# A five-stage pipeline for the weight conversion, with its sign mask in PSUM, and another order of the expert loop and the changeover

## Chip, core and metric

One core of a Trainium2 chip runs the whole program. The metric is device time in microseconds (us), the median over runs; less is better. TensorE (PE) multiplies matrices into PSUM; VectorE (DVE), ScalarE (ACT) and GpSimd (POOL) do elementwise work; SyncE (SP) issues most transfers. Each engine executes its own queue in order and waits for the others by semaphores.

## What is computed

Attention with queries averaged in pairs, then two feed-forward layers ("expert layers") on 1152 tokens of width 512, with 2048 hidden units. The reference, cut:

```python
q_pool = q.reshape(B, H, S // 2, 2, D).mean(axis=3)          # B=2, H=8, S=1152, D=64
attn = softmax(q_pool @ k^T / 8);  out = attn @ v
x = out as (1152 tokens, 512)
h = x @ w_in;   x = np.maximum(0.01 * h, h) @ w_out           # layer 0: 512 -> 2048 -> 512
h = x @ w_in2;  x = (h * np.tanh(softplus(h))) @ w_out2       # layer 1, same sizes
```

The four weight matrices arrive as 64-bit floats; everything else is 32-bit.

## The kernel before, in words

**Attention.** Eight pairs of heads, nine tiles of 128 queries each, so tiles 0 to 71. A tile n goes through scores on PE (tokens A, B, S, L263), maxima on DVE (M, N, K), the exponential on ACT (X, L290), three groups of transposes on PE (T, L311), and for each group a rounded copy on ACT (H, L319) and the remainder on DVE (L, L323). The product with the values (L339) ends in an ACT copy (L349), a small transfer and a POOL addition (L352). The queues' order is written out by hand, as strings of tokens: PATTERN for the first seven pairs, LAST for the eighth, TAIL behind it. PATTERN isn't touched. LAST and TAIL, the changeover, mix the last pair with the first expert work and the first weight blocks.

**Expert layers.** A layer takes its tokens in chunks of 512, 320 and 320 and, for each chunk, 16 hidden slices of 128. An iteration `it` (0 to 95) is one slice of one chunk: W, the in-projection, 12 matmuls into one of four PSUM banks (L552); u, two activations on ACT (L564, L565), of which one writes a rounded copy in a ring of three buffers and one rewrites the bank; y, a DVE subtraction that leaves the remainder (L567); O, the out-projection, 12 matmuls into four accumulators (L575). W reads X and the in-weights, O the u and y of its iteration and the out-weights. The string MOE says in which order one pass through the loop emits them: W(i), O(i-3), y(i-2), u(i), then Z, the copies at a chunk's end. u(i) writes the buffer that O(i-3) reads, so it waits for O(i-3).

**Weight conversion (class Conv).** 64 blocks of 128 x 512 weights, 32 per layer, in the order in which W and O need them. Per block: a 512 KB load (SP, L464); `ca`, two ACT instructions that take the high and the low word apart (L475, L476); `cv`, two DVE instructions that cut out the sign bit (L488) and put it on the shifted high word (L490); `cm`, a POOL addition of the low word (L503); `ch`, a rounded copy on ACT (L515); `cl`, the remainder, on DVE or POOL (L523). A "tick" emits the next step of each. Blocks 0 to 7 (`i < NA`) use one set of scratch buffers in I, later ones another in F. RATE says how many ticks a pass emits in the three stretches where blocks are converted: chunk 0 of layer 0 (2.25 a pass), chunk 2 of layer 0 (1.5, already for layer 1, whose weights overwrite layer 0's), chunk 0 of layer 1 (1).

The ring of buffers for late blocks, and the test for the start of a block:

```python
return tail[0], itmp[2 + i % 2], tail[1 + i % 2]          # one y, two k, two a
if i >= self.loaded or i > self.vecs or (self.merged < i if i < NA else self.merged < i - 1):
    return
```

Of the kernel before, what the change touches and what calls it, by code (L numbers as in the profile page):

```python
# [28 lines left out]
NA = 8  # L29
RATE = (2, 2.25, 1.5, 1)  # L30
# [11 lines left out]
    "B2 P70 X1 T00 P50 A2 H00 T20 H20 M2 S2 L00 T01 S3 A3 B3 N2 T10 H01 L20 K2 H10 T11 pv L01 X2 T21 L10 H21 T22 M3 N3 A4 K3 H22 L21 B4 H11 X3 L22 M4 T02 T12 H02 S4 H12 B5 L02 T23 L12 cf A5 H23 T03 L11 P20 N4 P120 K4 P30 ca P10 X4 cv c M5 P10 S6 H03 L23 ca T13 ch cp S5",  # L42
    "T11 L00 N2 T01 H01 H11 A3 B3 cv K2 X2 L01 T21 M3 N3 H21 H10 L21 cm L10 A4 B4 S4 ca ch cp T22 H22 L11 E0 P80 K3 P70 cv c X3 L22 P40 T02 H02 M4 N4 L02 T12 K4 T13 A5 H12 ca cv H13 ch T03 L13 cl L12 S5 X4 B5 H03 M5 N5 T23 c T14 ch cp ca H14 cv K5 L03 H23 W cm X5 T05 ch cp L14 ca L23 H05 cv c ch E0 P180 cl P10 T04 W T24 H04 L04 L05 T15 ca u c H15 T25 I5 H25 ch cp L25 ca u cv cm W ch cp H24 y W u B6 y L15 P190 W K6 R L24 M6 S6 O u A6 y X6 O N6",
    "A4 N4 K4 M4 S4 B4",
]
TAIL = "ca cv W ca cv u c cm ch y cl ca O cv ch cm cl y W ca u cv ch cl cm ca cv ch cl Y O u ca c cm ch cl ca cv ch cm cl"
MOE = "W O y u Z"
# [3 lines left out]
def tile_attention_moe_moe(  # L51
# [18 lines left out]
    F = sb.tile([128, 6432], F32, name="F")  # L70
# [186 lines left out]

    def emit_s(n, which):
        p = n // 9
        ops = q_ops(n)  # L260
# [27 lines left out]
    def emit_x(n):  # L288
        a, e = S_ALL[n % 2]
        nc.scalar.activation(out=ebuf[n % 3], in_=PS[:, a:e], func=AF.Exp, scale=SCALE,  # L290
                             bias=mx[:, n % 3, 2:3], accum_out=rcol(n))

    t_free, t_src = [0, 1, 2], {}
# [13 lines left out]
    def emit_t(n, g):  # L307
        bank, col = t_take()
        for i in range(3):
# [20 lines left out]
    def pv_ops(p, u):  # L330
# [40 lines left out]
    def last_recip():  # L371
        for first, c0, n in ((True, 0, 256), (False, 256, 320)):
# [17 lines left out]
    def pair_end_ops(p):  # L390
# [5 lines left out]
        def part(c0, n, first):  # L396
            bank, col = t_take()
# [30 lines left out]
    class Conv:  # L428


        def __init__(self):
            self.blocks = by_need(0) + by_need(1)
            self.loaded = self.acts = self.vecs = self.merged = self.highs = self.lows = 0
# [16 lines left out]
        def load(self):  # L450
            while self.loaded < len(self.blocks):
                i = self.loaded
                used = min(self.acts, self.vecs)
                if i < NA:
                    free = i - 2 < used
                elif i < NA + 3:
                    free = used >= NA and (i < NA + 2 or self.lows >= NA)
                else:
                    free = i - 3 < used
                if not free:  # L460
                    return
# [4 lines left out]
                self.loaded += 1  # L466

        def begin_act(self):
            i = self.acts
            if i >= self.loaded or i > self.vecs or (self.merged < i if i < NA else self.merged < i - 1):  # L470
                return
            y, k, a = self.bufs(i)
            if wide:
                v = self.raw(i).rearrange("p (n t) -> p n t", t=2)
# [3 lines left out]
            self.acts += 1  # L478

        def begin_vec(self):  # L480
            i = self.vecs
            if i >= self.acts or i - 2 >= self.lows:
                return
            y, k, a = self.bufs(i)
            if wide:
                ai = a.bitcast(I32)
                high = self.raw(i).rearrange("p (n t) -> p n t", t=2)[:, :, 1]
# [256 lines left out]
```

## Time and profile before

| | us |
|---|---|
| median of 3 runs | 694.49 (693.28 to 694.6) |
| profiled execution | 694.62 |
| its span, first to last instruction | 692.8 |
| PE busy / DVE busy / ACT busy / POOL busy | 659.6 / 442.8 / 428.7 / 280.8 |

The attention takes about the first 262 us, the expert layers the rest. A busy PE is not PE at its peak: matmuls are pipelined, and a row of 12 that waits in its middle shows as longer. The distance between the starts of two rows of PE says more: a W or an O of 12 matmuls takes 2.72 us for 512 tokens and 1.76 us for 320 where nothing holds it.

### The profile page before, as it was taken

What the parts mean: (1) busy time and instruction counts of PE and PEld (TensorE: products, weight loads), DVE (VectorE), ACT (ScalarE), POOL (GpSimd) and SP (SyncE); (2) the same over time, 40 slices, a digit from 0 to 9 for tenths busy, and PEclk for the clock granted to TensorE, in tenths of its full rate; (3) what the DMA queues carried; (4) which work ended last, traced back from release to release, by engine and by line L of the source; (5) the groups of instructions that cost most, each with busy time, mean ns of one, the idle gap of its engine ahead of it and who ended that gap; (6) DMA issues with size and microseconds to landing.
All of it is one profiled execution on the core that took longest, in us unless ns stands there. A gap on an engine that the chain in (4) does not pass through costs nothing. (4 is left out here: it accounts for less than half of the span.)

```text
span 692.8 us, 11045 instructions
## 1 busy us (share of the span) xinstructions
PE 659.6 (95%) x4048; PEld 599.3 (86%) x4048; DVE 442.8 (64%) x784; ACT 428.7 (62%) x851; POOL 280.8 (41%) x239
## 2 busy tenths in 40 slices
PE   2999999999999989989989999998999999999997
PEld 1899999999999867867768999998788889999997
DVE  5889999999999897499993111499975622111111
ACT  4989999898999797668773222477965422222221
POOL 6768577686857356465550000055532200000000
PEclk9999999999999999999999999999999999999999
DMA  6233232323322233355550000055532101001001
GB/s 170 73 83 115 81 105 90 82 80 84 114 78 52 70 115 113 111 167 183 182 184 28 1 1 1 31 184 183 167 137 91 31 1 61 1 1 39 1 1 39
DMA packets 18167, 57.74 MB, mean 83 GB/s; under 512 B 2368, under 2 KB 5440, under 8 KB 18112
## 3 DMA queue, kind: packets, MB, share of 16 engines
q1 hardware_dynamic: 16992, 52.44, 23.3%
q0 software_dynamic: 1120, 4.59, 2.9%
q8 instruction: 32, 0.52, 0.3%
q14 instruction: 23, 0.19, 0.1%
HBM read 47.71 MB, written 2.36 MB: 72 GB/s over the span
## 5 line engine op out<-in xcount | busy, mean ns | idle before, releaser
L575 PE MATMUL PS<-R 128*128 128x320 f32 (+1 forms) x1152 | 219.7, 339 | 7.5 <-DVE R L567 5.3
L552 PE MATMUL PS<-R 128*128 128x320 f32 (+1 forms) x1152 | 219.2, 339 | 1.2 <-ACT R L515 0.6
L575 PEld LDWEIGHTS PS<-R 128*128 128x128 f32 x1152 | 186.3, 188 | 28.5 <-DVE R L567 6.8
L552 PEld LDWEIGHTS PS<-R 128*128 128x128 f32 x1152 | 189.2, 190 | 18.3 <-DVE R L523 1.7
L564 ACT ACTIVATE R<-PS 128x320 fp32r<-128x320 f32 (+1 forms) x96 | 46.9, 489 | 187.8 <-PE PS L575 168.9
L503 POOL TENSOR_TENSOR F<-F,I 128x512 int32<-128x512 int32 x56 | 86.1, 1537 | 178.5 <-DVE F L490 174.2
L567 DVE TENSOR_TENSOR R<-PS,R 128x320 fp32r<-128x320 f32 (+1 forms) x96 | 52.6, 553 | 134.3 <-ACT PS L565 130.7
L263 PE MATMUL PS<-R 128*128 128x512 f32 (+2 forms) x480 | 110.5, 360 | 14.4 <-DVE R L213 9.5
L323 DVE TENSOR_TENSOR R<-PS,R 128x384 fp32r<-128x384 f32 x216 | 113.3, 550 | 11.2 <-ACT R L319 7.6
L319 ACT CAST R<-PS 128x384 fp32r<-128x384 f32 x216 | 95.0, 489 | 13.8 <-PE PS L311 11.9
L311 PE MATMUL PS<-F 128*128 128x128 f32 x648 | 95.1, 275 | 5.4 <-DVE R L323 4.1
L263 PEld LDWEIGHTS PS<-R 128*128 128x128 f32 x480 | 76.2, 193 | 22.9 <-issue 13.7
L290 ACT ACTIVATE F<-PS,F 128x1152 f32<-128x1152 f32 x72 | 88.6, 1231 | 10.1 <-PE PS L263 5.7
L339 PE MATMUL PS<-R 128*128 128x256 f32 (+1 forms) x576 | 93.8, 304 | 0.3 <-ACT R L319 0.2
L311 PEld LDWEIGHTS PS<-F 128*128 128x128 f32 x648 | 76.6, 140 | 15.4 <-DVE R L323 4.8
L339 PEld LDWEIGHTS PS<-R 128*128 128x128 f32 x576 | 80.0, 189 | 1.8 <-DVE R L323 0.5
L271 DVE TENSOR_REDUCE F<-PS 128x1 f32<-128x896 f32 x72 | 77.9, 1082 | 4.3 <-PE PS L263 4.3
L137 POOL TENSOR_TENSOR R<-I,R 64x1152 fp32r<-64x1152 f32 (+1 forms) x28 | 57.3, 2047 | 1.6
L523 DVE TENSOR_TENSOR R<-F,R 128x512 fp32r<-128x512 f32 x56 | 48.2, 860 | 14.7 <-ACT R L515 14.5
L488 DVE TENSOR_SCALAR F<-I 128x512 int32<-128x512 int32 x56 | 55.1, 984 | 2.8 <-POOL F L352 2.0
L490 DVE SCALAR_TENSOR_TENSOR F<-F 128x512 int32<-128x512 int32 x56 | 41.0, 733 | 24.7 <-ACT F L475 19.8
L352 POOL TENSOR_TENSOR F<-F 64x256 f32<-64x256 f32 (+1 forms) x32 | 25.9, 808 | 56.5 <-DMA F<-F 29.2
(75 smaller groups left out, 464.2 us busy)
## 6 DMA issues: line engine op xcount, KB each, us to landing
I<-in_w_dram SPq DMA_DIRECT2D x64, 512.0 KB, 3.3
I<-in_vN_dram SPq DMA_DIRECT2D x8, 576.0 KB, 4.2
R<-R POOLq DMA_DIRECT2D x14, 320.0 KB, 4.2
I<-in_qT_dram SPq DMA_DIRECT2D x7, 576.0 KB, 4.8
I<-in_kT_dram SPq DMA_DIRECT2D x7, 576.0 KB, 4.0
F<-F SPq DMA_DIRECT2D x16, 80.0 KB, 2.0
out_dram<-I SPq DMA_DIRECT2D x8, 160.0 KB, 2.0
F<-F SPq DMA_DIRECT2D x16, 64.0 KB, 1.9
```

The costliest lines, as they stand in the source:

```text
L137: nc.gpsimd.tensor_tensor(out=out, in0=src, in1=rounded(top), op=ALU.subtract)
L263: nc.tensor.matmul(out=PS[:, pc:pc + w], lhsT=lq, rhs=KS[p % 2][:, h, kc:kc + w], start=(i == 0), stop=(i == len(ops) - 1))
L271: nc.vector.tensor_reduce(out=mx[:, n % 3, 0:1], in_=PS[:, a:e], axis=AX.X, op=ALU.max, negate=True)
L290: nc.scalar.activation(out=ebuf[n % 3], in_=PS[:, a:e], func=AF.Exp, scale=SCALE, bias=mx[:, n % 3, 2:3], accum_out=rcol(n))
L311: nc.tensor.transpose(PS[:, col + 128 * i:col + 128 * i + 128], ebuf[n % 3][:, 128 * k:128 * k + 128], ident)
L319: nc.scalar.copy(out=pt_dst(n, g, 0), in_=t_src[n, g][1])
L323: nc.vector.tensor_tensor(out=pt_dst(n, g, 1), in0=src, in1=rounded(pt_dst(n, g, 0)), op=ALU.subtract)
L339: nc.tensor.matmul(out=PS[:, bank[1]:bank[1] + n], lhsT=vs[:, k, 128 * h:128 * h + 128], rhs=PT[:, slot, s, k, 0:n], start=(k == 0 and s = ...
L488: nc.vector.tensor_scalar(out=ai, in0=high, scalar1=-2 ** 31, scalar2=None, op0=ALU.bitwise_and)
L503: nc.gpsimd.tensor_tensor(out=a.bitcast(I32), in0=a.bitcast(I32), in1=k.bitcast(I32), op=ALU.add)
L552: nc.tensor.matmul(out=out, lhsT=wi[:, ws, k, fs], rhs=X[:, xs, k, tk], start=(k == 0 and i == 0), stop=(k == KD - 1 and i == 2))
L575: nc.tensor.matmul(out=PS[:, ACC[d]:ACC[d] + w], lhsT=wo[:, ws, f % FPS, 128 * d:128 * d + 128], rhs=G[:, it % 3, gs, 0:w], start=(f == 0 ...
```

## The change

Conv becomes one `step(what)` for five stages (act, vec, merge, high, low; the tokens ca, cv, cm, ch, cl now mean one step each), with a table of free buffers. A tick runs the stages from the last to the first, so each stage in a tick works on another block. Late blocks have two y, three k and four a buffers, in the place of the attention's exponentials. From block 10 on the sign bit (L533 in the new code) is written to PSUM bank 3, and the following instruction (L535) reads it there; the in-projection then rotates over three banks. LAST, TAIL and MOE have another order, and RATE is counted in half passes: 2, 1.25 and 1.2 ticks a pass. Weights of slices 4 to 7 and expert steps on blocks from 8 on are held back until the attention's end. `after()` and PT_FREE only assert an order while the program is built; they emit nothing.

```diff
-RATE = (2, 2.25, 1.5, 1)
+RATE = (1, 0.625, 0.6)
...
-MOE = "W O y u Z"
+MOE = "W O Z u t y t"
...
-    tail = [F[:, 800 + i * 512:1312 + i * 512] for i in range(3)]
+    cy = [F[:, 2976 + i * 512:3488 + i * 512] for i in range(2)]
+    ck = [F[:, 4000 + i * 512:4512 + i * 512] for i in range(3)]
+    signs = PS[:, 1536:2048].bitcast(I32)
+    ca = [F[:, 5536:6048], F[:, 6432:6944], itmp[2], itmp[3]]
...
-            return tail[0], itmp[2 + i % 2], tail[1 + i % 2]
+            j = i - NA
+            return cy[j % 2], ck[j % 3], ca[j % 4]
+        def free(self, i, what):
+            d = self.done
+            used = min(d["act"], d["vec"])
+            early = {"load": (2, used), "act": (1, min(d["vec"], d["merge"])), "vec": (2, d["low"])}
+            late = {"load": (3, used), "act": (2, min(d["vec"], d["merge"] + 1)), "vec": (4, d["low"])}
+            if what not in early:
+                return True
+            if i >= NA:
+                n, given = late[what]
+                if what == "load" and i < NA + 3:
+                    return given >= NA and (i < NA + 2 or d["low"] >= NA)
+                if what == "act" and t_count[0] < 3 * NT or what == "vec" and i > NA + 1 and d["merge"] < NA:
+                    return False
+                return i < NA + n or i - n < given
+            n, given = early[what]
+            return i - n < given
...
-                nc.vector.tensor_scalar(out=ai, in0=high, scalar1=-2 ** 31, scalar2=None,
+                sign = signs if cnt["y"] > 3 else ai
+                nc.vector.tensor_scalar(out=sign, in0=v[:, :, 1], scalar1=-2 ** 31, scalar2=None,
                                         op0=ALU.bitwise_and)
-                nc.vector.scalar_tensor_tensor(out=ai, in0=y.bitcast(I32), scalar=3, in1=ai,
+                nc.vector.scalar_tensor_tensor(out=ai, in0=y.bitcast(I32), scalar=3, in1=sign,
                                                op0=ALU.logical_shift_left, op1=ALU.bitwise_or)
...
         def tick(self):
             self.load()
-            self.begin_act()
-            self.begin_vec()
-            self.high()
-            self.merge()
-            self.low(nc.vector)
+            for what in reversed(self.STAGES):
+                self.step(what)
...
-    HB = [0, 512, 1024, 1536]
+    def h_bank(it):
+        return 512 * (it % 4 if it <= 4 else (it - 4) % 3)
...
+            if it >= (cnt["y"] + (4 if it <= 4 else 3) if t == "W" else cnt[{"u": "W", "y": "u", "O": "y"}[t]]):
+                return
+            parts = {"W": (0, 1), "O": (2 + ITS[it][2] % FPS,)}.get(t, ())
+            if not conv.open and any(conv.index(it, b) >= max(NA, conv.lows) for b in parts):
+                return
```

**What moves: DVE in a pass of chunk 0 of layer 0.** First the kernel before, then the changed one, each from a y on (L567 and L602 are y; L488/L490 and L533/L535 are cv; L523 and L552 are cl).

```order
L567 TENSOR_TENSOR R<-PS,R 128x512
L488 TENSOR_SCALAR F<-I 128x512
L490 SCALAR_TENSOR_TENSOR F<-F 128x512
L523 TENSOR_TENSOR R<-F,R 128x512
L488 TENSOR_SCALAR F<-I 128x512
```

```order
L602 TENSOR_TENSOR R<-PS,R 128x512
L552 TENSOR_TENSOR R<-F,R 128x512
L533 TENSOR_SCALAR PS<-I 128x512
L535 SCALAR_TENSOR_TENSOR F<-F,PS 128x512
L552 TENSOR_TENSOR R<-I,R 128x512
```

Two blocks a pass in both; now cl (of an older block) stands ahead of cv, and the sign goes through PS.

**ACT at tiles 67 to 69 of the last pair**, before and changed. L290 and L306 are the exponential, L349 and L373 the copies of the value products, L319 and L342 the rounded copies H, L475/L476 and L528/L529 the pair ca, L515 and L549 ch, L407 and L436 the end of the pair before.

```order
L290 ACTIVATE F<-PS,F 128x1152
L349 COPY F<-PS 128x256
L319 CAST R<-PS 128x3x128
L475 ACTIVATE I<-I 128x512
L476 ACTIVATE I<-I 128x512
...
L407 CAST R<-F 128x256
L290 ACTIVATE F<-PS,F 128x1152
L349 COPY F<-PS 128x320
L319 CAST R<-PS 128x3x128 x2
L475 ACTIVATE I<-I 128x512
L476 ACTIVATE I<-I 128x512
```

```order
L306 ACTIVATE F<-PS,F 128x1152
L528 ACTIVATE I<-I 128x512
L529 ACTIVATE I<-I 128x512
L373 COPY F<-PS 128x256
L342 CAST R<-PS 128x3x128
...
L436 CAST R<-F 128x256
L528 ACTIVATE I<-I 128x512
L529 ACTIVATE I<-I 128x512
L306 ACTIVATE F<-PS,F 128x1152
L373 COPY F<-PS 128x320
L342 CAST R<-PS 128x3x128 x3
```

ca of block 1 now stands ahead of the first of these copies, and ca of block 3 ahead of the exponential of tile 69.

**ACT at the end of the attention**, before and changed, from the copy of the last value product (L349, L373) to the first late blocks. L380 and L407 copy the reciprocals, L564/L565 and L599/L600 are u.

```order
L349 COPY F<-PS 128x256
L380 COPY F<-PS 128x256
L380 COPY F<-PS 128x320
L564 ACTIVATE R<-PS 128x512
L565 ACTIVATE PS<-PS 128x512
L475 ACTIVATE F<-I 128x512
L476 ACTIVATE I<-I 128x512
```

```order
L373 COPY F<-PS 128x256
L528 ACTIVATE I<-I 128x512
L529 ACTIVATE I<-I 128x512
L407 COPY F<-PS 128x256
L407 COPY F<-PS 128x320
L528 ACTIVATE F<-I 128x512
L529 ACTIVATE F<-I 128x512
...
L549 CAST R<-I 128x512
L549 CAST R<-F 128x512
L599 ACTIVATE R<-PS 128x512
```

ca of blocks 7, 8 and 9 and ch of 7 and 8 now stand between that copy and u(3); ch of block 7, the weights of O(1), stood ahead of the copy before.

## Rows read from the trace of the kernel before

**Rows 1.** The page's busy time of PE, share and instructions.

```profile
PE 659.6 (95%) x4048; PEld 599.3 (86%) x4048; DVE 442.8 (64%) x784; ACT 428.7 (62%) x851; POOL 280.8 (41%) x239
```

**Rows 2.** The chain of waits: shares by line; start, us, what.

```profile
by line: PE PS L575 20.7%; PE PS L552 19.1%; DVE F L488 1.1%; DVE R L523 0.9%; POOL F L503 0.7%; issue 0.6%; DVE F L490 0.5%; ACT R L564 0.3%; DVE R L567 0.2%; ACT L564 0.2%; ACT F L475 0.1%; ACT R L515 0.1%; ACT I L476 0.1%; ACTq L740 0.1%
...
380.31 1.76 PE PS L552 x12
...
507.77 2.72 PE PS L552 x12
```

**Rows 3.** Timeline of PE: start, us, what, [idle before <-releaser].

```profile
285.70 5.87 PE L575 MATMUL PS<-R 128*128 128x512 f32 x24
...
299.22 1.19 PE L552 MATMUL PS<-R 128*128 128x512 f32 x4 [0.30 <-DVE R L523]
...
357.28 1.92 PE L552 MATMUL PS<-R 128*128 128x320 f32 x12
...
364.03 1.66 PE L575 MATMUL PS<-R 128*128 128x512 f32 x4 [2.99 <-DVE R L567]
365.49 3.04 PE L552 MATMUL PS<-R 128*128 128x320 f32 x12
...
380.14 1.92 PE L552 MATMUL PS<-R 128*128 128x320 f32 x12
...
481.71 2.91 PE L552 MATMUL PS<-R 128*128 128x512 f32 x12
...
502.17 2.88 PE L552 MATMUL PS<-R 128*128 128x512 f32 x12
```

**Rows 4.** Windows: PE, PEld, DVE, ACT, POOL busy, granted clock, DMA share, GB/s.

```profile
318.00:345.00 27.00, 26.86 (x117) 21.25 (x116) 25.89 (x34) 21.72 (x39) 15.84 (x10) 1.00 0.56 187
...
364.00:368.00 4.00, 3.97 (x14) 3.66 (x15) 1.66 (x3) 1.30 (x4) 0.82 (x1) 0.57 0.28 110
...
461.00:496.00 35.00, 32.62 (x197) 30.09 (x196) 32.81 (x45) 28.71 (x53) 19.11 (x13) 1.00 0.55 182
```

**Rows 5.** Timeline of DVE, one pass of chunk 0, layer 0.

```profile
318.48 0.68 DVE L567 TENSOR_TENSOR R<-PS,R 128x512 fp32r<-128x512 f32 x1
319.08 0.93 DVE L488 TENSOR_SCALAR F<-I 128x512 int32<-128x512 int32 x1
320.11 0.69 DVE L490 SCALAR_TENSOR_TENSOR F<-F 128x512 int32<-128x512 int32 x1
320.72 0.68 DVE L523 TENSOR_TENSOR R<-F,R 128x512 fp32r<-128x512 f32 x1
321.44 1.40 DVE L488 TENSOR_SCALAR F<-I 128x512 int32<-128x512 int32 x1
...
324.16 0.69 DVE L567 TENSOR_TENSOR R<-PS,R 128x512 fp32r<-128x512 f32 x1
```

**Rows 6.** Timeline of POOL: cm of blocks 0, 2 and a late one.

```profile
245.41 1.28 POOL L503 TENSOR_TENSOR I<-I 128x512 int32<-128x512 int32 x1 [7.95 <-DVE I L490]
...
255.62 1.28 POOL L503 TENSOR_TENSOR I<-I 128x512 int32<-128x512 int32 x1
...
320.95 1.61 POOL L503 TENSOR_TENSOR F<-F,I 128x512 int32<-128x512 int32 x1 [1.23 <-DVE F L490]
```

**Rows 7.** Groups by shape: count, busy us, mean ns, idle before.

```profile
L475 ACT ACTIVATE F<-I 128x512 f32<-128x512 f32 x56 | 37.3, 666 | 9.5 <-DVE F L490 9.4
...
L488 DVE TENSOR_SCALAR I<-I 128x512 int32<-128x512 int32 x8 | 3.4, 420 | 0.0
```

**Rows 8.** Timeline of ACT in the changeover.

```profile
246.00 0.37 ACT L349 COPY F<-PS 128x256 f32<-128x256 f32 x1
...
253.67 1.23 ACT L290 ACTIVATE F<-PS,F 128x1152 f32<-128x1152 f32 x1
...
282.42 0.37 ACT L349 COPY F<-PS 128x256 f32<-128x256 f32 x1
```

**Rows 9.** The page's DMA issues: KB each, median us to landing.

```profile
I<-in_w_dram SPq DMA_DIRECT2D x64, 512.0 KB, 3.3
```

More of the change, by code (lines that the diff above doesn't have):

```diff
@@ L69, in tile_attention_moe_moe @@
     R = sb.tile([128, XW + WW + GW], F32R, name="R")
-    F = sb.tile([128, 6432], F32, name="F")
+    F = sb.tile([128, 6944], F32, name="F")
     I = sb.tile([128, 4096], I32, name="I")
@@ L256, in q_ops, with after @@
         return [(x[:, 1, 128 + 128 * t:256 + 128 * t], 1) for x in (a, w)]
+    given = set()
+    def after(*events, mark=None):
+        for e in events:
+            assert e in given or e[1] < 0, (e, mark)
+        given.add(mark)
     def emit_s(n, which):
         p = n // 9
+        after(("X", n - 2), mark=("S", n, which.start))
         ops = q_ops(n)
@@ L274, in emit_m2 @@
         a, e = S_SH[n % 2]
+        after(("S", n, 2), mark=("N", n))
         m = mx[:, n % 3]
@@ L289, in emit_x @@
         a, e = S_ALL[n % 2]
+        after(("K", n), *((("T", n - 3, g)) for g in range(3)), mark=("X", n))
         nc.scalar.activation(out=ebuf[n % 3], in_=PS[:, a:e], func=AF.Exp, scale=SCALE,
                              bias=mx[:, n % 3, 2:3], accum_out=rcol(n))
-    t_free, t_src = [0, 1, 2], {}
+    t_free, t_src, t_count = [0, 1, 2], {}, [0]
     def t_take():
@@ L307, in emit_t @@
     def emit_t(n, g):
+        after(("X", n), mark=("T", n, g))
         bank, col = t_take()
+        t_count[0] += 1
         for i in range(3):
@@ L358, in invert_sums @@
         rs, ri = rsum[p % 2], rinv[p % 2]
+        after(*(("X", 9 * p + j) for j in range(9)), mark=("I", p))
         rwide = rwides[p >= NPR - 2]
@@ L384, in last_end @@
         x = xu[(NPR - 1) % 2]
+        after(("R", 0), *(("U", NPR - 1, u) for u in range(4)), *(("E", NPR - 2, i) for i in (True, False)))
         xh, xl = (X[:, i, NPAIR - 1, SQ * (B - 1):SQ * B] for i in range(2))
@@ L396, in part @@
         def part(c0, n, first):
+            after(("I", p), ("U", p, 0), ("U", p, 1), ("U", p, 2), ("U", p, 3), mark=("E", p, first))
             bank, col = t_take()
@@ L450, in load @@
         def load(self):
[L451 to L460, printed above, removed]
+            while self.done["load"] < len(self.blocks):
+                i = self.done["load"]
+                if not self.free(i, "load"):
                     return
@@ L465, in load, with step @@
                                   in_=(w1, w2)[l][s, b].bitcast(I32))
[L466 to L470, printed above, removed]
+                self.done["load"] += 1
+        def step(self, what, eng=None):
+            i = self.done[what]
+            before = ("load", *self.STAGES)[self.STAGES.index(what)]
+            if i >= self.done[before] or not self.free(i, what):
                 return
             y, k, a = self.bufs(i)
-            if wide:
-                v = self.raw(i).rearrange("p (n t) -> p n t", t=2)
+            v = self.raw(i).rearrange("p (n t) -> p n t", t=2)
+            ai = a.bitcast(I32)
+            if what == "act" and wide:
                 nc.scalar.activation(out=y, in_=v[:, :, 1].bitcast(F32), func=AF.Copy, scale=2.0 ** -112)
@@ L518, in low @@
-        def low(self, eng):
-            i = self.lows
-            if i >= self.highs:
-                return
-            hi, lo = self.dst(i)
-            eng.tensor_tensor(out=lo, in0=self.bufs(i)[2], in1=rounded(hi), op=ALU.subtract)
-            self.lows += 1
+            elif what == "merge" and wide:
+                nc.gpsimd.tensor_tensor(out=ai, in0=ai, in1=k.bitcast(I32), op=ALU.add)
+            elif what == "high":
+                l, sl, b = self.blocks[i]
+                if sl > 3 and not self.open:
+                    return
+                if l == 1:
+                    f = sl * FPS + (FPS - 1 if b < 2 else b - 2)
+                    if cnt["W" if b < 2 else "O"] <= (NCHUNK - 1) * KF + f:
+                        return
+                nc.scalar.copy(out=self.dst(i)[0], in_=a)
+            elif what == "low":
+                hi, lo = self.dst(i)
+                (eng or nc.vector).tensor_tensor(out=lo, in0=a, in1=rounded(hi), op=ALU.subtract)
@@ L526, in tick, with index @@
+            self.done[what] += 1
+            if what == "vec":
+                self.load()
         def tick(self):
             self.load()
-            self.begin_act()
-            self.begin_vec()
-            self.high()
-            self.merge()
-            self.low(nc.vector)
+            for what in reversed(self.STAGES):
+                self.step(what)
+        def index(self, it, b):
+            l, c, f = ITS[it]
+            return self.blocks.index((l, f // FPS, b))
         def need(self, block):
```

81 lines of the change are left out of this document (33 added, 48 removed), and 3 rows, old and new, of the table LAST.

## Prediction

> **What bounds the kernel now.** I read the page's busy times first: PE is busy 95% of the span [rows 1], so a gain can only come from places where PE stands or crawls. The chain of waits says where: 40% of the span are the two matmul lines of the expert layers, and the rest of it is the weight conversion, L488, L523, L503 and L490, for about 4% [rows 2]. A row of 12 matmuls that nothing holds takes 2.72 us at 512 tokens and 1.76 us at 320 [rows 2]. With these I go along PE's timeline from the first O to the point from which the chain shows no more waits, and compare the distance between starts with that rate [rows 3]:
>
> - 285.70 to 357.28, which is O(0), O(1) and eleven passes of W and O at 5.44: 71.58 us for 65.28, lost 6.30. The row at 299.22 is typical; its W had run out of converted weights.
> - 357.28 to 365.49, W(16) and O(13): 8.21 for 4.48, lost 3.73. O(13) waits 2.99 us for a y, L567.
> - 365.49 to 380.14, two passes of 4.48 and one of 3.52: 14.65 for 12.48, lost 2.17. The granted clock is 0.57 from 364 to 368 [rows 4], so PE is at the lower level, 1.2 GHz, for some 3.4 us right after that wait; the rest is the end of chunk 0.
> - 380.14 to 481.71, 28 passes of 3.52: 101.57 for 98.56, lost 3.01.
> - 481.71 to 502.17, three passes of 4.48 and one of 5.44: 20.46 for 18.88, lost 1.58.
>
> Together 16.8 us. The windows name the culprit: DVE is busy 25.89 of 27 us from 318 to 345 and 32.81 of 35 from 461 to 496, ACT only 21.72 and 28.71 [rows 4]. DVE's timeline shows why [rows 5]. From y to y a pass with two blocks takes 324.16 - 318.48 = 5.68 us, more than PE's 5.44, and 2.25 blocks a pass are asked for. L488 takes 0.93 and 1.40 us there, although the same shape took 0.42 in the first eight blocks [rows 7]. It ends when POOL's addition of the block before ends: that ran from 320.95 to 322.56 [rows 6], L488 from 321.44 to 322.84 [rows 5]. So DVE's L488 and POOL's L503 don't run side by side; L488 waits.
>
> **The change, part by part.** *Sign mask in PSUM, and deeper buffers.* L533 writes PSUM and L535 reads one operand there. The trace has no DVE instruction that writes PSUM from SBUF. Its price lies between 0.42 (the mask alone) [rows 7] and 1.40 (the mask behind POOL) [rows 5]; I take 0.68, the subtraction L567 of the same width with an operand in PSUM [rows 5], and suppose that it no longer waits for POOL. From start to start a pass is then two times (0.71 mask with its gap to the next, 0.61 L490, 0.60 L523) and 0.60 for y: 4.44 us. With the ends of the price it is 3.9 and 5.9. DVE then has 1.0 us to spare in a pass of 5.44, PE bounds these passes, and y comes in time for O(13): nothing is late next on DVE. ACT was busy 21.72 of 27 us at more than two blocks a pass [rows 4] and gets two, so it isn't next either. W now needs the y of three passes ago instead of four, and that y stands two passes ahead of it in DVE's queue. A load takes 3.3 us [rows 9], its buffer comes free a pass ahead. I leave 0.5 us for this stretch.
>
> L523 still takes two operands from SBUF, and POOL's L503 starts right behind L490, where L523 comes now too. The row shows who wins: L523 at 320.72 took its 0.68, and L503, issued at 320.95, was stretched from 1.28 to 1.61 [rows 5, 6]. The Trainium skill's page "SBUF — State Buffer", section "SBUF: two separate sides", states that the port pair of DVE and GpSimd is an exclusive lock which the first comer keeps for a whole instruction, also against a DVE instruction with two SBUF inputs. By that rule an L523 that comes late loses a whole L503; this is a rival below.
>
> *Rates and loop order.* In chunk 2 of layer 0 a pass of 3.52 us gets 1.25 blocks instead of 1.5: DVE needs 1.25 x 1.92 + 0.4 = 2.8 us instead of 1.5 x 2.54 (half of 5.68 - 0.60) + 0.4 = 4.2. Of the 3.01 and 1.58 us I leave 0.5 and 0.4. In chunk 0 of layer 1 the rate goes up to 1.2, 2.9 us of DVE beside 5.44 of PE, hidden. Z now stands ahead of u: its copies free the accumulators about one u earlier. Of the 2.17 the clock's part goes with its cause, and I leave 0.5 for both chunk ends.
>
> *Start of the late blocks.* Before, ch(7) stood ahead of the last value product's copy at 282.42 [rows 8], and load 8 ahead of that copy's transfer. Now ca(7), then ca(8), ca(9) and ch(7) follow the copy on ACT, and load 8 follows its transfer on SP. Load 8 can be issued at 282.8 and lands at 286.1; the copies of the reciprocals come on ACT until 286.2; ca(8) takes 1.2 (two of 0.67, overlapping) [rows 7], to 287.4. Load 9 waits for cv(7) at about 284.7, lands at 288.0, ca(9) ends at 289.2, ch(7) at 289.8. O(1), which needs ch(7), would start at 285.70 + 2.72 = 288.42: PE stands 1.4, and cl(7) behind ch(7) adds 0.2. Then ca(10) to ca(12) stand ahead of u(5) and ch(10), so W(6) waits again, 0.8, where it waited before too. Sum 2.4; it could be 0 if loads land together, and 3.7 if cl(7) loses a whole 1.28 [rows 6] to POOL.
>
> *Changeover.* Two pairs ca move up on ACT. ca(1) now stands ahead of the copy at 246.00 [rows 8], and its second half needs the k buffer that cm(0) reads until 246.69 [rows 6]: the copy comes at 247.35, 1.35 later, and with it a transpose, H, L and K of tile 68. ca(3) stands ahead of the exponential of tile 69, at 253.67 before [rows 8]. Its second half waits for cm(2), which ended at 256.90 [rows 6]; what is queued behind the waiting ca(3) on ACT is that exponential, and PE's transposes and scores wait for it. By these rows it starts at about 256.90 + 0.65 + 0.9 (what is left of the delay before) = 258.4, 4.7 later. The value product of 18 matmuls hides a part, and PE and DVE, which stood there for each other before, catch up on another part. So the loss lies between 0 and 4.7; followed instruction by instruction W(0) comes 2.4 later, which I take. A gain is excluded up to tile 69, since everything there comes later or as before.
>
> *Sum.* PE's losses behind 285.70 go from 16.8 to 0.5 + 0.5 + 0.4 + 0.5 + 2.4 = 4.3, a gain of 12.5. The changeover costs 2.4. Net -10.1, on the profiled execution's 694.62: **684.5 us**. That execution is 0.13 above the median of the runs shown, which I neglect; 1.8 us lie outside its span and stay.
>
> **The rivals.**
> - *The changeover takes more.* The whole 4.7 comes through, O(1) and W(6) cost 3.7, and the pause brings one more stretch at the lower clock, 1.7: losses 7.3 instead of 4.3, net -4.8, **690**. For it: one wait of 2.99 was followed by such a stretch [rows 3, 4].
> - *The changeover is free.* Loads land early, and tile 69's delay falls into waits that were there: losses 1.9, net -14.9, **680**.
> - *The depth isn't used.* ch and ca still come in one bunch behind u, which waits for O; passes stay at 5.68, 2.2 more, O(13) still waits 2, chunk 2 keeps its 3.0 and layer 1 its 1.6: losses 11.7, net -2.7, **692**. Against it: ACT's idle fifth [rows 4].
> - *Slower: DVE stays the bound.* If each L523 finds POOL at work, or if the PSUM write costs as much more, a block pays up to 1.28 more: a pass takes 7.0, nine passes lose 14, chunk 2 (1.25 x 3.2 + 0.4 = 4.4 for 3.52, fourteen passes, 5 us of it hidden by y's lead) loses 7; losses 24.3, net +9.9, **704**. The gain is gone from about 1.0 us per block on. Against it: the 0.68 of the row at 320.72 [rows 5]. By the page named above this is what a late L523 pays, and the trace agrees where L488 paid it.
>
> **How the numbers follow.** Forecast 0.62, with its own range of 681 to 688; changeover dearer 0.16; free 0.10; depth unused 0.07; slower 0.05. Leaving out the last two and the end of the free case leaves out under 0.2: the range is 680.3 to 690. A measurement of this kernel can tell some 0.2% from no change, 1.4 us. Faster by more than that: forecast, dearer, free and most of the unused depth, 0.92; same 0.03; slower 0.05.
>
> **What would show it.** Right: W starts 5.44 apart from W(7) to W(15); the 2.99 wait of O(13) and the clock stretch behind it are gone; DVE below 0.9 busy there; L533 near 0.68 whether POOL works or not; a wait of 1 to 3 us at O(1) for ACT's ch(7); the exponential of tile 69 starting 3 us or more later. Wrong: passes of 5.7 or more with DVE full, L523 above 1.2, or L533 near 1.4; a first W at 262 or earlier would take the changeover's loss away.

## The result, and the profile after

The changed kernel takes **685.0 us** (684.69 to 685.6) where the kernel before takes 693.91 (693.28 to 694.6): a ratio of 0.9873, with a 95% interval of 0.9855 to 0.989. The forecast was 684.5. The profiled execution took 685.6, its span is 683.8, 9.0 under the one before.

TensorE is now busy 96% of the span. For the same 4048 instructions it is busy 5.9 us less than in [rows 1], so a part of its busy time before was slow work: the W at 365.49 took 3.04 us [rows 3], a W of this width takes 1.92 in the rows below.

```profile
PE 653.7 (96%) x4048; PEld 598.5 (88%) x4048; DVE 433.8 (63%) x786; ACT 426.6 (62%) x851; POOL 268.1 (39%) x237
```

In the changed kernel W is L587, O L610, u L599 and L600, y L602; cv is L533 (mask) and L535, cl L552, cm L540, ca L528 and L529, ch L549. First the timeline of PE at the places of [rows 3] and where it still waits (start, us, what, idle before and releaser):

```profile
287.35 3.05 PE L610 MATMUL PS<-R 128*128 128x512 f32 x12
291.97 1.20 PE L610 MATMUL PS<-R 128*128 128x512 f32 x4 [1.57 <-ACT R L549]
...
302.57 0.73 PE L587 MATMUL PS<-R 128*128 128x512 f32 x2 [0.59 <-ACT R L549]
304.09 1.20 PE L587 MATMUL PS<-R 128*128 128x512 f32 x4 [0.79 <-DVE R L552]
...
318.00 2.09 PE L610 MATMUL PS<-R 128*128 128x512 f32 x8 [0.76 <-DVE R L552]
...
358.01 1.92 PE L587 MATMUL PS<-R 128*128 128x320 f32 x12
359.77 2.91 PE L610 MATMUL PS<-R 128*128 128x512 f32 x12
362.51 1.92 PE L587 MATMUL PS<-R 128*128 128x320 f32 x12
...
374.19 1.59 PE L610 MATMUL PS<-R 128*128 128x320 f32 x9 [0.18 <-DVE R L621]
375.62 1.92 PE L587 MATMUL PS<-R 128*128 128x320 f32 x12
...
474.18 2.91 PE L587 MATMUL PS<-R 128*128 128x512 f32 x12
...
493.14 1.07 PE L587 MATMUL PS<-R 128*128 128x512 f32 x4
```

W(16) is at 358.01 and O(13), which waited 2.99 us before, follows it at 359.77 without a wait. From W(20), 375.62, to W(48), 474.18, are 98.56 us: exactly 28 free passes of 3.52. Apart from 0.18 us at 374.19, the waits that are left lie between O(1) and O(5).

The same windows as [rows 4]:

```profile
318.00:345.00 27.00, 27.00 (x119) 22.39 (x120) 25.96 (x36) 22.70 (x42) 15.65 (x11) 1.00 0.63 212
...
364.00:368.00 4.00, 4.00 (x22) 3.51 (x22) 0.97 (x2) 1.99 (x4) 1.30 (x1) 1.00 0.48 165
...
461.00:496.00 35.00, 35.00 (x200) 32.10 (x200) 31.09 (x44) 28.83 (x57) 14.16 (x11) 1.00 0.49 154
```

The clock from 364 to 368 is 1.00, the higher level of 2.4 GHz, where it was 0.57. PE is full in both stretches. But DVE is as full from 318 to 345 as before, 25.96 of 27 us. That was not forecast. Its timeline tells why, one pass from y to y, and POOL beside it:

```profile
326.64 0.68 DVE L602 TENSOR_TENSOR R<-PS,R 128x512 fp32r<-128x512 f32 x1
327.24 1.47 DVE L552 TENSOR_TENSOR R<-I,R 128x512 fp32r<-128x512 f32 x1
328.64 0.68 DVE L533 TENSOR_SCALAR PS<-I 128x512 int32<-128x512 int32 x1
329.43 0.69 DVE L535 SCALAR_TENSOR_TENSOR I<-F,PS 128x512 int32<-128x512 int32 x1
330.03 0.69 DVE L552 TENSOR_TENSOR R<-F,R 128x512 fp32r<-128x512 f32 x1
330.63 0.69 DVE L533 TENSOR_SCALAR PS<-I 128x512 int32<-128x512 int32 x1
331.43 0.69 DVE L535 SCALAR_TENSOR_TENSOR I<-F,PS 128x512 int32<-128x512 int32 x1
332.03 0.68 DVE L602 TENSOR_TENSOR R<-PS,R 128x512 fp32r<-128x512 f32 x1
```

```profile
326.87 1.30 POOL L540 TENSOR_TENSOR F<-F 128x512 int32<-128x512 int32 x1 [0.39 <-ACT F L528]
330.26 1.62 POOL L540 TENSOR_TENSOR I<-I,F 128x512 int32<-128x512 int32 x1 [2.09 <-DVE I L535]
```

The mask L533 takes 0.68 whatever POOL does (0.68 to 0.70 in all 54 that write PSUM). The first cl, L552, ends 0.5 us after POOL's addition that began at 326.87, and takes 1.47; the second one, at 330.03, was first, and there POOL pays (1.62 instead of 1.30). A pass is 5.39 us, against PE's 5.44.

At W(6) such a long cl holds PE. The W that goes on at 304.09 waits for this cl, which starts behind POOL's addition; with 0.69 it would have ended at 303.24, before PE had done the row of 302.57, so about 0.8 us there are POOL's (an estimate from these rows):

```profile
302.55 1.49 DVE L552 TENSOR_TENSOR R<-I,R 128x512 fp32r<-128x512 f32 x1 [0.49 <-ACT R L549]
```

```profile
302.20 1.28 POOL L540 TENSOR_TENSOR F<-F 128x512 int32<-128x512 int32 x1 [0.25 <-DVE F L535]
```

In the third chunk, too, cl is long. A pass with one block takes 467.77 - 464.45 = 3.32 us from y to y, one with two 473.02 - 467.77 = 5.25, against PE's 3.52:

```profile
464.45 0.48 DVE L602 TENSOR_TENSOR R<-PS,R 128x320 fp32r<-128x320 f32 x1
464.85 1.68 DVE L552 TENSOR_TENSOR R<-F,R 128x512 fp32r<-128x512 f32 x1
...
467.77 0.48 DVE L602 TENSOR_TENSOR R<-PS,R 128x320 fp32r<-128x320 f32 x1
...
473.02 0.48 DVE L602 TENSOR_TENSOR R<-PS,R 128x320 fp32r<-128x320 f32 x1
```

To compare all kernels, this table cuts PE's timeline at the starts of the same products. W(n) is the first W of the expert layers' pass n, counted from 0. "Free" is the rate of [rows 2]; from W(52) to the last O all kernels but the two with three banks in the old order agree within 0.02 us.

| kernel | O(0) at | O(0) to W(16) | W(16) to W(20) | W(20) to W(44) | W(44) to W(52) |
|---|---|---|---|---|---|
| free | | 65.28 | 16.96 | 84.48 | 32.96 |
| before | 285.70 | 71.58 | 22.86 | 84.88 | 37.14 |
| changed | 287.35 | 70.66 | 17.60 | 84.48 | 33.05 |

The 9.0 us are 1.65 lost up to O(0) and 0.92, 5.26, 0.40 and 4.09 won in the four stretches. The losses behind O(0) went from 16.8 to 6.1; 4.3 was forecast.

The first of these numbers is the least certain. Six of the kernels profiled here have the old order up to O(0), and their W(0) lies anywhere from 259.77 to 262.10; four have the changed one, with 264.26 to 264.94. On average W(0) comes 3.3 us later and O(0) 2.9; the two executions compared here show 2.16 and 1.65.

### The profile page after: what moved, and what is told of

The parts are those of the page before. It is cut to its first block, busy times and chain, and to the rows that moved or that the text cites. A ratio compares the mean times of both kernels' runs of the same rounds, so it can differ in the third digit from the quotient of the medians.

```text
span 683.8 us, 11018 instructions
## 1 busy us (share of the span) xinstructions
PE 653.7 (96%) x4048; PEld 598.5 (88%) x4048; DVE 433.8 (63%) x786; ACT 426.6 (62%) x851; POOL 268.1 (39%) x237
## 4 chain that ended last, share of the span: by engine, by line
PE 87%; DVE 3%; ACT 3%; DMA 3%; POOL 1%; issue 1%; SPq 0%; ACTq 0%; DVEq 0%; POOLq 0%
PE PS L587 27%; PE PS L610 27%; PE PS L275 12%; PE PS L363 11%; PE PS L329 10%; DMA I<-in_w_dram 2%; DVE R L216 1%; ACT F L528 1%; DMA I<-in_qT_dram 1%; ACT F L306 1%; POOL I L540 1%; DVE R L552 1%; DVE F L284 0%; DVE R L347 0%; PE PS L429 0%
## 5 line engine op out<-in xcount | busy, mean ns | idle before, releaser
L587 PE MATMUL PS<-R 128*128 128x320 f32 (+1 forms) x1152 | 217.6, 338 | 1.4 <-DVE R L552 0.8
L610 PE MATMUL PS<-R 128*128 128x320 f32 (+1 forms) x1152 | 216.2, 337 | 2.5 <-ACT R L549 1.6
L587 PEld LDWEIGHTS PS<-R 128*128 128x128 f32 x1152 | 188.2, 189 | 17.7 <-DVE R L552 1.2
L610 PEld LDWEIGHTS PS<-R 128*128 128x128 f32 x1152 | 186.7, 188 | 19.1 <-ACT R L549 2.2
L599 ACT ACTIVATE R<-PS 128x320 fp32r<-128x320 f32 (+1 forms) x96 | 47.2, 492 | 170.6 <-PE PS L610 146.0
L602 DVE TENSOR_TENSOR R<-PS,R 128x320 fp32r<-128x320 f32 (+1 forms) x96 | 52.8, 554 | 132.8 <-ACT PS L600 129.2
L347 DVE TENSOR_TENSOR R<-PS,R 128x384 fp32r<-128x384 f32 x216 | 113.3, 549 | 15.8 <-ACT R L342 14.7
L342 ACT CAST R<-PS 128x384 fp32r<-128x384 f32 x216 | 94.7, 489 | 15.9 <-PE PS L329 14.2
L306 ACT ACTIVATE F<-PS,F 128x1152 f32<-128x1152 f32 x72 | 88.5, 1230 | 7.8 <-PE PS L275 4.2
L540 POOL TENSOR_TENSOR F<-F 128x512 int32<-128x512 int32 x28 | 38.5, 1376 | 120.0 <-DVE F L535 116.6
L540 POOL TENSOR_TENSOR I<-I,F 128x512 int32<-128x512 int32 x28 | 38.2, 1366 | 45.1 <-DVE I L535 38.9
L528 ACT ACTIVATE F<-I 128x512 f32<-128x512 f32 x56 | 37.7, 673 | 17.3 <-DMA I<-in_w_dram 5.6
L600 ACT ACTIVATE PS<-PS 128x320 f32<-128x320 f32 (+1 forms) x96 | 46.9, 488 | 0.0
```

Source lines behind the costliest of these rows:

```text
L347: nc.vector.tensor_tensor(out=pt_dst(n, g, 1), in0=src, in1=rounded(pt_dst(n, g, 0)), op=ALU.subtract)
L540: nc.gpsimd.tensor_tensor(out=ai, in0=ai, in1=k.bitcast(I32), op=ALU.add)
L587: nc.tensor.matmul(out=out, lhsT=wi[:, ws, k, fs], rhs=X[:, xs, k, tk], start=(k == 0 and i == 0), stop=(k == KD - 1 and i == 2))
L602: nc.vector.tensor_tensor(out=gl, in0=h, in1=rounded(gh), op=ALU.subtract)
L610: nc.tensor.matmul(out=PS[:, ACC[d]:ACC[d] + w], lhsT=wo[:, ws, f % FPS, 128 * d:128 * d + 128], rhs=G[:, it % 3, gs, 0:w], start=(f == 0 ...
```

## The experiments

**The mask back in SBUF** (a1_mask_sbuf), all else as changed:

```
-                sign = signs if cnt["y"] > 3 else ai
+                sign = ai
```

> The changed kernel with one thing undone: the sign mask of every block is written to SBUF again, as before; buffers, tick order, banks and rates stay. Theory (the gain comes from a DVE that no longer waits for POOL in the mask): the mask goes from 0.685 us back to about 1.0 us, DVE needs 2 x 2.7 + 0.6 = 6.0 us for a pass of 5.44, the passes of chunk 0 stretch to 5.7 or more, and the time is 688 to 692. Rival (the deeper buffers and the reversed tick bring the gain, the place of the mask hardly matters): within 1 us of the changed kernel's 685.0, and passes of 5.44.

Measured: 692.65 us (690.53 to 695.14), ratio to the kernel before 0.9982 (0.9967 to 0.9997). O(0) is at 287.47, and only O(0) to W(16) differs from the changed kernel: 77.69 for 70.66. DVE's timeline, one pass from y to y, cut:

```profile
337.75 0.68 DVE L602 TENSOR_TENSOR R<-PS,R 128x512 fp32r<-128x512 f32 x1
338.35 1.48 DVE L552 TENSOR_TENSOR R<-F,R 128x512 fp32r<-128x512 f32 x1
339.75 0.42 DVE L533 TENSOR_SCALAR F<-I 128x512 int32<-128x512 int32 x1
...
341.49 1.53 DVE L533 TENSOR_SCALAR F<-I 128x512 int32<-128x512 int32 x1
...
343.73 0.68 DVE L602 TENSOR_TENSOR R<-PS,R 128x512 fp32r<-128x512 f32 x1
```

One mask of two pays 1.53 and one cl of two 1.48: y to y is 343.73 - 337.75 = 5.98 us, and PE follows DVE again. The theory was right, with 5.98 for 6.0; the time came 0.65 above its range. So the mask's place is worth 7.0 us, and all of it in chunk 0 of layer 0; what the change won in the third chunk does not come from it.

**The mask in PSUM alone** (b1_mask_psum). The kernel before with the mask in the fourth bank, W going round the other three from pass 5 on:

```
+                sign = signs if cnt["y"] > 3 else ai
-                nc.vector.tensor_scalar(out=ai, ...
+                nc.vector.tensor_scalar(out=sign, ...
...
-                nc.vector.scalar_tensor_tensor(... in1=ai,
+                nc.vector.scalar_tensor_tensor(... in1=sign,
...
-    HB = [0, 512, 1024, 1536]
+    def h_bank(it):
+        return 512 * (it % 4 if it <= 4 else (it - 4) % 3)
```

> The kernel before with one thing added: the sign mask goes to PSUM from block 10 on and the in-projection rotates over three banks; buffers, order and rates are as before. Theory (DVE's waits for POOL in the mask were the bound): the mask takes 0.69 us instead of 0.98, the wait of O(13) shrinks below 1.5 us, and the time is 686 to 690. Rival (depth and order bring the gain): 692 to 694, with the 3 us wait of O(13) still there.

Measured: 717.38 (714.17 to 720.78), ratio 1.0341 (1.0301 to 1.0381). Both theories missed: with the mask at 0.68 us it is 23.5 us *slower*. Its longest waits are W's for y, 3.69 us at 338.35, and neither the mask nor a full DVE explains them: from 300 to 366 us DVE is busy 0.83. Left to test was the lost bank:

**Three banks alone** (b3_three_banks), the same edit without the mask.

> The kernel before with one thing changed: from expert 5 on its in-projection goes round three PSUM banks instead of four; the sign mask stays in SBUF. Theory (the bank, not the mask, is what made the kernel before 23.5 us slower when it was given the mask in PSUM): 710 to 720 us, with TensorE in front of the in-projection waiting for the activation product y three banks back, 1 to 4 us at a time. Rival (the mask or its PSUM traffic is at fault there): 694 us plus or minus 1, and no such waits.

Measured: 715.46 (714.66 to 716.4), ratio 1.031 (1.029 to 1.033). It is the bank. PE, and who held y, L569 (ACT's L566 is u, L515 ch):

```profile
311.21 4.48 PE L554 MATMUL PS<-R 128*128 128x512 f32 x12 [3.75 <-DVE R L569]
...
339.18 5.46 PE L554 MATMUL PS<-R 128*128 128x512 f32 x12 [3.34 <-DVE R L569]
```

```profile
336.79 0.62 ACT L515 CAST R<-F 128x512 fp32r<-128x512 f32 x1 [0.50 <-POOL F L503]
337.31 0.59 ACT L566 ACTIVATE R<-PS 128x512 fp32r<-128x512 f32 x1
...
338.36 0.68 DVE L569 TENSOR_TENSOR R<-PS,R 128x512 fp32r<-128x512 f32 x1
```

W waits for a y that stands on DVE behind the instructions of three blocks, from 329.97 to 338.36, and its u on ACT behind a ch that waits for POOL. The clock falls too: from 339 to 344 us 0.50 is granted, the lower level, and the row of the W behind the 3.34 us wait takes 5.46, where that of a free W takes 2.88. The bank costs wherever blocks are converted: W(20) to W(44) takes 91.88 for 84.88, W(44) to W(52) 44.33 for 37.14. In the changed kernel no row of PE waits for y, so three banks cost nothing that its rows show.

O(0) to W(16), from before to changed, is thus: one bank less +12.80 (84.38), the new stages and order -6.69 (a1's 77.69), the mask out of SBUF -7.03 (70.66). The -6.69 holds the lower rate of chunk 0 as well, 2 blocks a pass for 2.25; three banks at that rate in the old order, and four banks in the new one, were not run. In the old order the mask in PSUM is worth 3.2 us of this stretch (b1's 81.17 for 84.38).

**The old rates in the changed kernel** (a5_old_rates):

```
-RATE = (1, 0.625, 0.6)
+RATE = (1.125, 0.75, 0.5)
```

> The changed kernel with the conversion rates of the kernel before (1.125, 0.75 and 0.5 blocks per expert for the three chunks in place of 1, 0.625 and 0.6). Theory (the rates, not the place of the mask, took the losses out of layer 0's last chunks): losses come back there, of the 2 to 3 us that the kernel before lost in them, time 687 to 688 us. Rival (the order of the five stages took them out): 685 us plus or minus 0.7, TensorE full between 461 and 496 us.

Measured: 694.28 (692.76 to 695.29), ratio 1.0005 (0.9992 to 1.0018): the whole gain is gone. W(44) to W(52) takes 40.20 for 33.05; the other stretches agree within 0.5. The theory was right and its size three to four times too small. The losses are larger than those of the kernel before at the same rates (37.14): the changed kernel needs the lower rates more than the old one did; whether for its three banks or its long cl was not taken apart. PE waits for y in every second or third pass and then for the chunk-end copy:

```profile
465.39 2.02 PE L587 MATMUL PS<-R 128*128 128x320 f32 x12 [1.08 <-DVE R L602]
...
473.93 2.02 PE L587 MATMUL PS<-R 128*128 128x320 f32 x12 [1.25 <-DVE R L602]
...
497.46 3.53 PE L610 MATMUL PS<-R 128*128 128x512 f32 x12 [1.81 <-DVE R L621]
```

**The new rates in the kernel before** (b4_new_rates):

```
-RATE = (2, 2.25, 1.5, 1)
+RATE = (2, 2.25, 1.25, 1.2)
```

> The kernel before with the rates of the changed one in the last two stages alone (1.25 blocks per expert in layer 0's third chunk in place of 1.5, 1.2 in layer 1's first chunk in place of 1). Theory (the old kernel's losses there, 3.0 and 1.6 us, are a matter of rates by themselves): most of them go, 690 to 691 us. Rival (the one-bank-in-three rotation and the new stages are what the rates were cut for; the kernel before gains nothing from them): 693.5 us plus or minus 0.7.

Measured: 689.42 (689.07 to 690.61), ratio 0.9947 (0.9931 to 0.9962). W(44) to W(52) is 33.05, as in the changed kernel; all else is as before, the 3.03 us wait of O(13) too. So the 4.09 us are the rates' of the last two stretches; the lower rate in chunk 0 was not tried here.

**The copies first** (b2_z_first), in the kernel before:

```
-MOE = "W O y u Z"
+MOE = "W O Z y u"
```

> The kernel before with the copies at a chunk's end (Z) ahead of the activations u and y in the loop. Theory (the value product of the next chunk waits for the accumulators, and the copies stand behind u and y): the crawl at the ends of chunks in layer 0 shrinks by 1 to 1.5 us, 692 to 693 us. Rival (the copies ahead delay u and y, and the next expert's product with them, by as much): 693.5 us plus or minus 0.7.

Measured: 692.17 (690.4 to 692.38), ratio 0.9972 (0.9958 to 0.9986). W(16) to W(20) is 20.96 for 22.86, W(20) to W(44) 84.48 for 84.88 and W(44) to W(52) 36.51 for 37.14. O(13) still waits 3.04 us, but in this profile no stretch at the lower clock followed it. The profiled execution took 690.53, 1.6 below the median, so the 20.96 is not what most of its runs show.

**Both** (b5_rates_z).

> The kernel before with two edits of one line each: the new rates of the last two stages (alone: 4.0 us faster) and the chunk-end copies ahead of y and u (alone: 1.2 us faster). Theory (the two repair different places, the end of chunk 0 and the third chunk): the gains add, 688.2 us plus or minus 0.7, so that the stages, the PSUM mask and the bank rotation together bring the remaining 3 us of the change. Rival (both shorten the same waits, at the changes of chunk): 689.4 us or more.

Measured: 689.23 (687.31 to 689.86), ratio 0.992 (0.9892 to 0.9948). The two ratios above multiply to 0.9919, so the gains would add; but the medians lie only 0.2 apart from the rates alone, and the interval holds both answers. Not decided. In the trace W(16) to W(20) is 22.50 for 22.86, and the lower clock is back behind O(13). Windows of this kernel, then of the one with the copies first:

```profile
364.00:368.00 4.00, 3.81 (x15) 3.62 (x16) 1.33 (x3) 1.46 (x4) 0.97 (x1) 0.67 0.32 118
```

```profile
364.00:368.00 4.00, 4.00 (x23) 3.62 (x22) 0.08 (x1) 0.42 (x2) 0.00 (x0) 1.00 0.04 14
```

**Two ca moved back** (a2_ca_back). The changed kernel with ca of blocks 1 and 3 in their old places, behind the copy and behind the exponential of tile 69:

```
-... cl X4 S6 cv c P10 ...
+... cl X4 S6 cv cm P10 ...
-... P70 cv c X3 ... H02 ca T13 L02 T12 K4 cl A5 cv H12 ca H13 ...
+... P70 cv cl cm X3 ... H02 T13 L02 T12 K4 cl A5 H12 ca cv H13 ...
```

> The changed kernel with one thing undone: in the last pair the pairs ca of block 1 and of block 3 stand on ACT where they stood before, behind the copy of the value product and behind the exponential of tile 69. Theory (they hold up that copy and that exponential while they wait for the k buffer): the exponential of tile 69 starts near 253.7 again instead of 256.94, the first W near 262.1 instead of 264.26, and the time is 682.5 to 683.5. Rival (DVE bounds the changeover, the delay only fills its waits): the first W moves by less than 0.7 us and the time stays within 0.7 us of 685.0.

Measured: 682.17 (681.5 to 683.55), ratio 0.9836 (0.9815 to 0.9856). The theory was right: the exponential of tile 69 starts at 253.81, W(0) comes at 261.46 for 264.26 and O(0) at 284.09 for 287.35; the rest is as in the changed kernel. What the changeover cost is in this row of ACT in the changed kernel, with the exponential behind it:

```profile
256.38 0.66 ACT L529 ACTIVATE I<-I 128x512 int32<-128x512 uint32 x1 [1.73 <-POOL I L540]
256.94 1.21 ACT L306 ACTIVATE F<-PS,F 128x1152 f32<-128x1152 f32 x1
```

**Without POOL's addition** (a4_no_merge):

```
-            elif what == "merge" and wide:
+            elif what == "merge" and wide and i < NA:
```

> The changed kernel without the low-word addition on GpSimd (cm) for blocks 8 and later: this part of the computation is left out, so the sums of those blocks lack the low words. Theory (the DVE operation cl takes 1.47 us in place of 0.69 in each second pass because GpSimd's addition holds the shared port when it starts): mean of cl in the chunk after the changeover falls from 1.07 us to 0.66 to 0.72, the DVE pass from 5.4 to 4.6 us, the 0.76 us wait at the sixth expert goes and most of the 1.4 us at the seventh, time 683 us plus or minus 1. Rival (cl waits for something else, its sources or the PSUM): cl stays at 1.0 us or more and the time at 685.

Measured: 684.02 (683.93 to 685.41), ratio 0.9866 (0.985 to 0.9882). From 300 to 358 us every cl takes its own time (groups by shape: count, busy, mean ns):

```profile
L552 DVE TENSOR_TENSOR R<-I,R 128x512 fp32r<-128x512 f32 x11 | 7.5, 687 | 1.9 <-ACT R L549 1.9
...
L552 DVE TENSOR_TENSOR R<-F,R 128x512 fp32r<-128x512 f32 x10 | 6.9, 687 | 4.1 <-ACT R L549 4.1
```

So POOL's addition is what stretches cl, as the theory said, and without it a pass takes 4.6 us from y to y where DVE sets it. The losses at W(6) and O(5) shrink from 2.0 and 1.2 to 0.7 and 0.5, and O(0) to W(16) falls to 68.42, but O(0) came 1.85 later in this run and the time hardly moved. This run takes away the contention and a step of the chain cv, cm, ch, cl at once, so by itself it can't say which of the two the waits were.

**Another changeover** (a6_changeover). As with the two ca moved back, and from the last tile on all conversions written in another order, in LAST (not shown) and TAIL, load 8 and block 7 early:

```
-TAIL = "cm y y cl W cv cp y u ch cv cl cm O ca ca W c cv y ca ca ca cm W W ...
+TAIL = "ch cl W ca u ch cl cv cm O ca cv cm y u ch cl W ch ca cv cm cl ca cv ...
```

> The changed kernel with ca of blocks 1 and 3 as before, and the end of the changeover in another order: ca and cv of block 7 ahead of the last value product's copy (so that loads 8 and 9 go out before its transfer), ch and cl of block 7 right behind it, and the steps of blocks 8 to 15 spread between the expert steps. Theory (O(1) waits for load 8 and W(6) for blocks that start late): the wait of 1.57 us at O(1) is gone, those at W(6) shrink from 1.4 to under 0.5, and with the earlier exponential the time is 679.5 to 681.5. Rival (the late blocks wait for DVE anyway, wherever they start): the waits move to W(6) to W(8) in the same sum, and the time is 682.5 to 683.5.

Measured: 685.44 (683.93 to 688.11), ratio 0.9884 (0.9855 to 0.9914). O(1)'s wait is gone, but the last value product waits 3.37 for a DVE instruction (L347) that now stands behind conversions, O(0) is at 290.62, and later passes wait 1.70 and 0.93 for cl. The wait moved, as the rival said, but to the last value product, which it did not name, and the time is above both ranges.

**Only block 7 early** (a7_load8_early). As with the two ca moved back, with these steps added:

```
-... y L15 P190 S6 W K6 R M6 L24 O O u A6 y X6 N6
+... y L15 ca cv cm P190 S6 cl W K6 R M6 L24 O ch cl ca cv ca cm cv ch cm O u A6 y X6 N6
```

> The changed kernel with the two absolute values ahead of the changeover back in their old places, and in addition block 7's absolute value, mask and addition put ahead of the last value product's copy, with the loads of blocks 8 and 9 ahead of its transfer. Theory (the second expert waits 1.8 us because the conversions that the first two experts bring start only then): that wait goes, time 680 to 681 us. Rival (the wait only moves, to the last value product or to the sixth to eighth expert, as in the first trial of another order): 682 us or more.

Measured: **679.88** (678.12 to 680.81), ratio 0.9798 (0.9779 to 0.9818), faster than both kernels. O(0) is at 284.33, and O(1) follows without a wait, 2.86 later. What still waits on PE:

```profile
297.40 0.73 PE L587 MATMUL PS<-R 128*128 128x512 f32 x2 [0.54 <-ACT R L549]
298.78 1.21 PE L587 MATMUL PS<-R 128*128 128x512 f32 x4 [0.64 <-DVE R L552]
...
311.31 1.20 PE L610 MATMUL PS<-R 128*128 128x512 f32 x4 [0.41 <-ACT R L549]
313.05 2.11 PE L610 MATMUL PS<-R 128*128 128x512 f32 x8 [0.55 <-DVE R L552]
```

**y behind cl** (a8_y_behind_cl). On top of that, y is issued between cl and the rest of its tick, so that a cl, not y, follows each L535:

```
-MOE = "W O Z u t y t"
+MOE = "W O Z u ty t"
```

> The version with block 7 converted early, with one more edit: in the expert loop the activation product y comes behind the first low-word subtraction cl of its tick instead of ahead of it, so that a cl follows each bitwise step cv at once and GpSimd's addition cm starts after it. Theory (cl takes 1.47 us in each second pass because y lets cm take the shared port first): cl falls from 1.05 to 1.07 us to 0.69 to 0.8 mean, the DVE pass from 5.4 to about 4.6 us, and most of the 2 us of waits between the sixth and eighth experts and at the fifth value product go: 678 us plus or minus 1. Rival (those waits come from the late start of the conversion, not from the length of a DVE pass, or y comes late instead and three banks make TensorE wait for it): 680 us or more.

Measured: 681.74 (681.02 to 682.88), ratio 0.9834 (0.9817 to 0.9852). From 314 to 353 us twelve of fifteen cl take 0.69, three 1.23 to 1.77; the mean is 0.84 for 1.05. Where cl is first, POOL pays. DVE and POOL:

```profile
316.51 0.69 DVE L535 SCALAR_TENSOR_TENSOR I<-F,PS 128x512 int32<-128x512 int32 x1
317.12 0.69 DVE L552 TENSOR_TENSOR R<-F,R 128x512 fp32r<-128x512 f32 x1
```

```profile
317.35 1.62 POOL L540 TENSOR_TENSOR I<-I,F 128x512 int32<-128x512 int32 x1 [0.98 <-DVE I L535]
```

But the waits at W(6) and O(5) stand as they were (0.51 and 0.65, 0.45 and 0.68), O(0) to W(16) is 68.85 for 68.75, and nothing is won; the rival's time was right. Its cause is not shown by this: up to O(5) the long cl are as long as without the edit (1.79 and 1.12 us for 1.78 and 1.12), so the edit did not shorten the passes ahead of these waits. The cl that W(6) and O(5) wait for take 0.69 in both kernels. Here these waits are for a cl that starts late, behind its ch; the long cl at W(6) is the changed kernel's own, with its wait of 0.79. What would let them start earlier was not tried.

## Why the prediction was right, and where it was not

The total was right within 0.5 us of the median, in part by luck: behind O(0) 1.8 us more were lost than forecast, and the changeover cost 0.75 less in the profiled execution. From profile to profile the gain is 9.0, where 10.1 was forecast. Its main mechanism held: the mask no longer waits for POOL, PE bounds the steady passes, and the wait of O(13) is gone. What it had wrong is the price of cl, and how late the first late blocks are.

- **The mask's price** was right: 0.68 taken, 0.685 on average over all 54 of them, with and without POOL beside it. That POOL no longer matters to it was a supposition, and it held.
- **The pass of 4.44 us** was wrong: 5.39, and DVE is busy 0.96 of that stretch, not below 0.9. The step that failed is the one that gave L523's successor 0.60 in every block, from a row in which it was first (that row has 0.72 to the next start, but 0.60 is what a free cl takes now). In the new order y stands ahead of every second cl, so POOL's addition starts before it, and that cl pays 0.8 us more, what was a rival of 0.05; its cl of 1.47 is above the 1.2 that the prediction named as a sign of being wrong. The mask's step, 0.79 to the next start for 0.71, is most of the rest. The Trainium skill's page "SBUF — State Buffer", section "SBUF: two separate sides", says that whichever of the two starts first holds the port pair for the whole instruction. The rows above agree in both directions, 1.47 for cl behind POOL and 1.62 for POOL behind cl, and the rule should have been applied to the new order, not only priced as a rival. In the steady passes it did no harm by a margin of 0.05 us, which is luck: the rival named 1.0 us a block as the point from which the gain is gone, and what came in chunk 0 is 0.4. At W(6) it cost about 0.8.
- **Start of the late blocks** was right in place and too small: O(1) lost 1.9 (1.6 forecast), W(6) 2.0 (0.8), of which about 0.8 is the long cl, and O(5) 1.2 that was not named; its cl takes 0.69 and starts late. Together with the passes, O(0) to W(16) lost 5.4 where 2.9 was forecast.
- **O(13) and the clock** went as forecast: W(16) to W(20) lost 0.6 for 0.5. The reason given was a DVE pass with 1.0 us to spare, which it hasn't. The wait is gone with the mask in SBUF as well (17.60), and with the old rates (18.10), so it went with the stages and the order, which were not taken apart.
- **The rates** were right in what they leave lost, 0.1 for 0.9, and wrong in the price of a block: 3.32 and 5.25 us for a pass with one and with two, where 1.92 a block and 0.4 give 2.3 and 4.2. By these rows four passes with five blocks need 15.2 us of DVE beside 14.1 of PE; what hid the difference is not shown, so that the small loss is luck too. Six blocks, the old rate, need 17.1, and the changed kernel with the old rates takes 16.93 for the four passes from W(44) to W(48). So here the rate, and not a shorter pass, took the losses away; it is worth 4.1 us in the old kernel and 7.2 in the changed one, in W(44) to W(52).
- **The changeover** was right: W(0) 2.16 later for 2.4 in the profiled execution (3.3 on average over the kernels with this order), the exponential 3.27 for 4.7. The copy at 246.00 was not held up: cm(0) began at 244.21, 1.2 us earlier than in [rows 6], and ca waited for it 0.19.
- **A share** was misread: L488, L523, L503 and L490 have 3.2% of the chain in [rows 2], not about 4%; nothing in the sum rests on it.
- **What was not seen:** what one PSUM bank less costs. The prediction left 0.5 us for it, and in the changed kernel no wait for y shows. In the old order it costs 22, more than the mask brings, so that the mask and the bank only pay with the new order and rates.

## To carry over

Before taking a buffer away from a loop, look at what stands ahead of the instruction that frees it, on each in-order queue: here one bank of four cost 22 us in the old kernel and nothing that shows in the changed one. Where two engines hold each other up, as cl and POOL's addition do here, follow the order of their starts through one pass of the new order: the one that started second paid, 1.47 for 0.69 or 1.62 for 1.30. And price the one-line edits of a large change apart: the rates alone gave 4.0 of the 8.9 us, and without them the changed kernel gains nothing.

## What the chip showed that was not expected

- The same wait of 3.0 us of O(13) was followed by the lower clock in the profiles of the kernel before (0.57 granted, [rows 4]), of the one with new rates (0.57) and with both edits (0.67), and not in the one with the copies first (1.00). One profile each: a wait of this length does not always bring it. Nor is it a matter of the kernel alone: of the ten runs with the copies first, three with a mean granted clock of 0.998 to 1.000 took 690.40 to 690.75 us, seven with 0.991 to 0.996 took 691.83 to 692.38.
- An int32 mask from SBUF to PSUM took 685 ns at 512 elements beside a busy POOL, while the same one within SBUF took about 420 when first and 930 to 1540 when not (984 on average in the kernel before): the slower form is the better one where POOL works.
